# Attention, experts and a bilinear layer: the loop over further windows moved to the end of the program, with a buffer cleared ahead of the experts

## The chip, the cores and the metric

The kernel runs on one core of a Trainium2 chip. The metric is the device time of one execution in microseconds. The core's engines are named here as the profile names them: PE is TensorE, PEld its weight load, DVE is VectorE, ACT ScalarE, POOL GpSimd, SP SyncE, which issues most of the transfers.

## The reference

```python
# attention: batch 2, 8 heads, 768 tokens, 64 dims, 16 clusters
q_assign = np.argmax(np.einsum('bhsd,hcd->bhsc', q_n, c_n), axis=-1)
k_assign = np.argmax(np.einsum('bhsd,hcd->bhsc', k_n, c_n), axis=-1)
mask = q_assign[:, :, :, None] == k_assign[:, :, None, :]
scores = scale * np.matmul(q, k.transpose(0, 1, 3, 2))
scores = np.where(mask, scores, -1000000000.0)
...
return np.matmul(attn, v).astype(np.float32)

# experts: x [1536, 512], w_gate [512, 8], w1 [8, 512, 1024], w2 [8, 1024, 512]
logits = x @ w_gate
expert_idx = np.argmax(logits, axis=1)
...
for e in range(E):
    mask = expert_idx == e
    xe = x[mask]
    h = np.maximum(xe @ w1[e], 0.0)
    ye = h @ w2[e]
    out[mask] = gate_w[mask, None] * ye

# bilinear layer: w_a, w_b [512, 1536], w_out [1536, 512]
a = x @ w_a
b = x @ w_b
return (a * b @ w_out).astype(np.float32)
```

## The kernel before

Three stages follow one another. The attention takes up to about 295 us. The experts take from there to 520 us, the bilinear layer from 526 us to the end. Every product runs as three products of float32r parts: high by high, high by low, low by high. So each weight chunk is loaded (`piece_load`, L97), for the last layer turned from 64-bit into 32-bit words by three VectorE instructions (`piece_bits`, L120 to L124), and then split (`piece_parts`): `hi` is a cast on ScalarE (L137), `lo` a subtraction `raw - hi` (L141), for every second chunk on GpSimd, for the others on VectorE. NRAW staging tiles `raw` take turns; a load waits until the `lo` that read the tile before it is done.

The tokens of each expert stand in a region of their own of `xs` in DRAM. GpSimd puts them there by indirect scatters (L508). An expert's first 256 tokens are one window (`window`, L961 on): eight blocks of hidden units, each 12 matmuls into one of three banks `h` (L968), then `hh` by ScalarE (L972) and `hl` by VectorE (L973), which reads the bank last and so frees it for the block three further on; then 96 matmuls `y` (L983) with the second weight. Chunks 0 to 3 of an expert are its first weight, two blocks to a chunk, 4 to 7 its second. Between the blocks, `tick` lets other work be put into the engines' queues, in the order in which the program is written: the next splits (`advance`), and, in the first window, steps of `tables` on VectorE (L600 to L694), which count tokens and make the tables of windows. `store` (L991, L992) copies `y` to its tokens' columns in `yt`, which holds all tokens' rows, transposed, for the last layer: 4 x 1792 float32 in each partition.

An expert with more than 256 tokens has further windows of 128 rows. The first of them, over all experts, is worked off by `spill` within the row of experts. Any others are taken by a loop on the device, `tc.For_i(0, nv)` (L1158), between the experts and the bilinear layer, one window to a pass, written into `yt`. With the inputs timed here the experts have 198, 119, 169, 188, 162, 192, 206 and 302 tokens, so there is one further window, `spill` takes it, and `nv` is 0. Ahead of the loop two small matmuls are issued (`keep_warm`, L701).

The bilinear layer splits columns of `yt` into `yh` and `yl` (L1212 and L1214, L1218), multiplies by `w_a` and `w_b` into `ab` (L1242), multiplies the two into `ga` (L1249), splits that into `gh` and `gl` (L1250, L1251) and multiplies by `w_out` into `o` (L1265). Rows of the result, scaled by the gate (L1273), are scattered to their tokens' places in `out` (L1276) by GpSimd.

Within an engine instructions run in the order in which they were issued. Between engines they wait for semaphores, which the framework places where tiles are read and written, or where a tile's memory was used by another before.

Of the kernel before, what the change touches and what calls it, by code (L numbers as in the profile page):

```python
# [8 lines left out]
F32 = mybir.dt.float32  # L9
# [15 lines left out]
WS = 128  # L25
# [4 lines left out]
def cluster_attention__then__moe__then__bilinear_kernel(  # L30
# [37 lines left out]
    # ---- weights in chunks of [128, 1024], each split into two float32r parts  # L68
# [7 lines left out]
    # A piece is what one staging tile holds: a chunk of w1 (256 columns) or of  # L76
    # w2 (256 rows), or half a chunk of w_a, w_b or w_out, which come as float64
    # and are read as pairs of 32-bit words.
# [25 lines left out]

    def piece_bits(n):
        """First part of a split: float64 to float32."""
        t = raw_t.pop(n)
        i, j = pieces[n]
        if j == 0:
            s = i % NSLOT  # L110
            pn = pools["a" if s < NA else "b"]
            hi_t[i] = pn.tile([128, CH], F32R, tag=f"hi{s}", name=f"hi_{i}")
            lo_t[i] = pn.tile([128, CH], F32R, tag=f"lo{s}", name=f"lo_{i}")
        if i >= MOE2:
            # float64 to float32: sign and top exponent bit stay, the other three
            # bits by which the exponents differ go, the fraction is cut to 23 bits
            # (exact for zeros, and to 24 bits in float32's normal range)
            r = t.rearrange("p (f w) -> p f w", w=2)
            tmp = pools["b"].tile([128, CH // 2], U32, tag="tmp", name=f"tmp_{n}", bufs=2)
            nc.vector.tensor_scalar(out=tmp, in0=r[:, :, 1], scalar1=5, scalar2=2,  # L120
                                    op0=ALU.logical_shift_left, op1=ALU.logical_shift_right)
            nc.vector.scalar_tensor_tensor(out=tmp, in0=r[:, :, 1], scalar=0xC0000000, in1=tmp,  # L122
                                           op0=ALU.bitwise_and, op1=ALU.bitwise_or)
            nc.vector.scalar_tensor_tensor(out=tmp, in0=r[:, :, 0], scalar=29, in1=tmp,  # L124
                                           op0=ALU.logical_shift_right, op1=ALU.bitwise_or)
            t = tmp
        bits_t[n] = t.bitcast(F32)

    def piece_parts(n, hi_eng, lo_eng):
        """Second part of a split: high and low float32r."""  # L130
# [16 lines left out]
    # ---- scratch in DRAM: a region of S*B rows for each expert  # L147
# [4 lines left out]
    # ---- constants of the routing  # L152
# [121 lines left out]
    # centroids over their norms, laid out as a block diagonal for each head pair  # L274
# [31 lines left out]
    # The norm of a query or key row scales its similarities by one positive  # L306
    # factor, so it does not change which centroid has the largest one.
    class Prep:
        """The steps that lay out the operands of a pair of heads."""
# [17 lines left out]
        def sims(self, tag="X", bufs=1):  # L327
            # similarities, transposed: row 32 g + 16 h + c
# [29 lines left out]
        def rows(self, nm, tag="X", bufs=1, copies=(act_copy, dve_copy, act_copy, dve_copy)):  # L358
            # cluster rows of the queries, penalty rows of the keys
# [21 lines left out]
        def high(self, nm, h, i, other, copy):  # L381
            """High parts: those of head h, in stack i, own half or (keys) the other one."""
# [63 lines left out]
    def pv_steps(p, g, j0=0, nj=NG, tags=("O", "X"), per=1):  # L446
        """Values times probabilities for nj query tiles of a group, in steps."""
# [22 lines left out]
    def emit_x(p, t0, nj, ot, sm, tag):  # L470
        b, hp = pairs[p]
        if hp == 0 and t0 == 0:
            xb[b] = xpool.tile([128, NT, DM], F32, name=f"x{b}")
            lg[b] = xpool.tile([128, NT, E], F32, name=f"lg{b}")
# [21 lines left out]
    # =========================== routing ===========================  # L496
# [4 lines left out]
    def apart(group, inst, why):  # L501
        """Scatters of a group go to rows of their own: none waits for another."""
# [104 lines left out]
        # the expert with the most tokens, and where its further window starts  # L607
# [21 lines left out]
        # all windows beyond the first, one to a partition  # L629
# [28 lines left out]
        # start of each window inside its expert, then the three columns of the table  # L658
# [16 lines left out]
        # where the tokens go: number and squared gate of each  # L675
# [135 lines left out]
    def place_split(t, c0, c1, copy):  # L811
        """Columns of tile t in two float32r parts."""
# [11 lines left out]
    def place_mm(t, d):  # L824
        """Adds the tokens of tile t to the transposed rows of the first window."""
# [75 lines left out]
    # =========================== experts ===========================  # L901
    st_yt = ExitStack()
    ytp = pool(ctx, "yt")
    yt = ytp.tile([128, DB, NTOK + W], F32, name="yt")
    pb = pool(ctx, "chunks_b")
# [7 lines left out]
    def advance(n, engines, later=0):  # L913
        """Splits up to piece n, of the last ones only the first part, and loads."""
# [31 lines left out]
    def win_xt(w, n, a):  # L946
        """Transposes of the rows 128 a ... of a window, and their split."""
# [48 lines left out]
    def spill(w, c0, tick, nxt):  # L996
        """A window of 128 rows with the rows stationary; returns its last part."""
# [98 lines left out]
    # the first banks are those that the first window's rows are read from until late  # L1096
# [53 lines left out]
    keep_warm(2, "xt", [128, 512], 2, mps)  # L1150
    st_me.close()

    # ---- any further windows, one at a time
    with ExitStack() as st:
        lp = pool(st, "loop")
        lps = pool(st, "loop_ps", space=PSUM)
        nv = nc.values_load(regs["ni"][0:1, 0:1], min_val=0, max_val=16, skip_runtime_bounds_check_because=why)
        with tc.For_i(0, nv) as it:  # L1158
            row = lp.tile([1, 4], I32, name="row")
            nc.sync.dma_start(out=row, in_=tab[bass.ds(it, 1)])  # L1160
            ev2 = sp_value(row[0:1, 0:1], E - 1)
            rv2 = sp_value(row[0:1, 1:2], E * NTOK - WS)
            dv2 = sp_value(row[0:1, 2:3], NTOK - WS)
            x1 = lp.tile([128, DM], F32, name="x1")
            nc.sync.dma_start(out=x1, in_=xs[bass.ds(rv2, WS)])
            x1t = lp.tile([128, DB, WS], F32, name="x1t")
            for d in range(DB):
                xp = lps.tile([128, 512], F32, tag="xp", name="xp")
                nc.tensor.transpose(xp[:, 0:128], x1[:, 128 * d:128 * d + 128], ident)
                nc.vector.tensor_copy(x1t[:, d, :], xp[:, 0:128])  # L1170
            h1 = lp.tile([128, FB, WS], F32, name="h1")
            for c in range(4):
                wt = lp.tile([128, DB, 256], F32, tag="wt", name="wt", bufs=2)
                nc.sync.dma_start(out=wt, in_=w1[bass.ds(ev2, 1), :, 256 * c:256 * c + 256].rearrange(
                    "e (k p) f -> p (e k) f", p=128))
                for j in range(2):
                    hp_ = lps.tile([128, 512], F32, tag="xp", name="hp")
                    for d in range(DB):
                        nc.tensor.matmul(hp_[:, 0:WS], lhsT=wt[:, d, 128 * j:128 * j + 128], rhs=x1t[:, d, :],
                                         start=(d == 0), stop=(d == DB - 1))  # L1180
                    nc.scalar.activation(out=h1[:, 2 * c + j, :], in_=hp_[:, 0:WS], func=AF.Relu)
            y1 = [lps.tile([128, 512], F32, tag=f"y1{d}", name=f"y1{d}") for d in range(DB)]
            for c in range(4):
# [121 lines left out]
```

## Time and profile before

| | |
|---|---|
| median of 3 runs | 832.33 us (831.39 to 832.38) |
| span of the profiled execution | 830.4 us |
| PE busy | 793.5 us, 96% |
| DVE busy | 541.5 us, 65% |
| ACT busy | 367.1 us, 44% |
| POOL busy | 292.9 us, 35% |
| transfers | 81.91 MB, mean 99 GB/s |

The span runs from the first to the last instruction of one profiled execution; the time of a run is taken around it. A share is an average over all three stages.

### The profile page before, as it was taken

Reading aid. Unit: us, or ns where it says so; the run is one execution under the profiler, and the core shown is the slowest. Engines: PE = TensorE matmul, PEld = TensorE weight load, DVE = VectorE, ACT = ScalarE, POOL = GpSimd, SP = SyncE. Lnnn points to the kernel's source line nnn. Section 1 sums busy time; section 2 is a strip of 40 time slices with the busy share of each in tenths; the row PEclk is TensorE's granted clock in tenths of the full one; section 3 lists DMA queues with packets and bytes.
Section 4 is the critical chain, followed back from the end, with each engine's and each line's share of the span. In section 5 each row is a group of like instructions: output and inputs, shape, how many; then the busy total and the mean of one; then the engine's idle time right before and its main releaser. Section 6 shows DMA issues by size and latency. Waiting matters only on the chain. (4 is left out here: it accounts for less than half of the span.)

```text
span 830.4 us, 12569 instructions
## 1 busy us (share of the span) xinstructions
PE 793.5 (96%) x4832; PEld 639.1 (77%) x4832; DVE 541.5 (65%) x900; ACT 367.1 (44%) x693; POOL 292.9 (35%) x233
## 2 busy tenths in 40 slices
PE   8999999999999988899999999799999999999996
PEld 5666666665666778899999999588888888888885
DVE  6868879778786789555554459874565667624333
ACT  5867667766676454445564542222322212201100
POOL 4915434344540454576553334321121121101011
PEclk9999999999999999799999999899999999999998
DMA  9405012221100155768785654431131120001011
GB/s 299 97 1 159 1 39 63 64 58 45 52 20 1 50 197 167 225 148 221 230 276 184 218 183 153 117 114 51 51 93 60 51 70 32 1 0 51 1 51 51
DMA packets 69949, 81.91 MB, mean 99 GB/s; under 512 B 27264, under 2 KB 48256, under 8 KB 69888
## 3 DMA queue, kind: packets, MB, share of 16 engines
q1 hardware_dynamic: 67584, 74.78, 30.5%
q0 software_dynamic: 2304, 6.31, 2.0%
q8 instruction: 39, 0.64, 0.3%
q14 instruction: 22, 0.18, 0.1%
HBM read 70.58 MB, written 10.50 MB: 98 GB/s over the span
## 5 line engine op out<-in xcount | busy, mean ns | idle before, releaser
L141 POOL TENSOR_TENSOR lo<-raw,hi 128x1024 fp32r<-128x1024 f32 x37 | 92.7, 2509 | 88.8 <-ACT hi L137 43.6
L1242 PE MATMUL ab<-yh,hi 128*128 128x512 f32 x288 | 113.4, 394 | 6.0 <-ACT yh L1214 6.0
L141 POOL TENSOR_TENSOR lo<-tmp,hi 128x512 fp32r<-128x512 f32 x36 | 51.5, 1430 | 179.1 <-ACT hi L137 177.1
L1242 PE MATMUL ab<-yh,lo 128*128 128x512 f32 x288 | 113.1, 393 | 0.0
L1249 DVE TENSOR_TENSOR ga<-ga,ab 128x512 f32<-128x512 f32 x36 | 24.7, 685 | 127.3 <-PE ab L1242 104.4
L417 DVE TENSOR_REDUCE nm<-s 128x1 f32<-128x768 f32 x96 | 91.5, 953 | 17.9 <-PE s L415 12.4
L424 ACT ACTIVATE pr<-s,nm 128x768 f32<-128x768 f32 x96 | 87.2, 908 | 17.6 <-DVE nm L417 16.5
L438 PEld LDWEIGHTS t<-ident,pr 128*128 128x128 f32 x576 | 62.9, 140 | 40.6 <-ACT pr L424 16.8
L415 PE MATMUL s<-ks,qs 128*128 128x512 f32 (+1 forms) x384 | 91.2, 359 | 1.1 <-ACT pr L424 0.6
L438 PE MATMUL t<-ident,pr 128*128 128x128 f32 x576 | 83.8, 279 | 2.8 <-DVE pt L444 2.8
L1248 ACT COPY ga<-ab 128x512 f32<-128x512 f32 x36 | 21.1, 587 | 143.3 <-PE ab L1242 143.3
L453 PE MATMUL o<-pt,vn 128*64 128x384 f32 (+1 forms) x432 | 82.5, 472 | 0.0
L968 PE MATMUL h<-xh,hi 128*128 128x256 f32 x256 | 68.3, 297 | 10.2 <-DVE hl L973 10.0
L137 ACT CAST hi<-raw 128x1024 fp32r<-128x1024 f32 x70 | 72.4, 1047 | 12.6 <-DMA raw<-in_moe_w 12.5
L1242 PE MATMUL ab<-yl,hi 128*128 128x512 f32 x288 | 77.8, 392 | 0.0
L983 PE MATMUL y<-hh,hi 128*128 128x256 f32 x256 | 73.5, 287 | 0.0
L141 DVE TENSOR_TENSOR lo<-raw,hi 128x1024 fp32r<-128x1024 f32 x35 | 61.0, 1746 | 18.0 <-ACT hi L137 17.5
L983 PE MATMUL y<-hh,lo 128*128 128x256 f32 x256 | 72.4, 283 | 0.0
L983 PE MATMUL y<-hl,hi 128*128 128x256 f32 x256 | 72.4, 283 | 0.0
L442 ACT COPY pt<-t 128x384 f32<-128x384 f32 x98 | 46.9, 480 | 54.4 <-PE t L438 52.7
L1242 PEld LDWEIGHTS ab<-yh,hi 128*128 128x128 f32 x288 | 54.8, 190 | 17.6 <-ACT yh L1214 6.2
L415 PEld LDWEIGHTS s<-ks,qs 128*128 128x128 f32 x384 | 58.2, 189 | 12.1 <-issue 3.8
(309 smaller groups left out, 1682.3 us busy)
## 6 DMA issues: line engine op xcount, KB each, us to landing
raw<-in_moe_w SPq DMA_DIRECT2D x72, 512.0 KB, 4.6
raw<-in_moe_w_a SPq DMA_DIRECT2D x12, 512.0 KB, 3.7
raw<-in_moe_w_b SPq DMA_DIRECT2D x12, 512.0 KB, 3.7
raw<-in_moe_w_out SPq DMA_DIRECT2D x12, 512.0 KB, 3.3
xs<-zero SPq DMA_DIRECT2D x8, 512.0 KB, 5.2
xw<-xs SPq DMA_DIRECT2D x15, 256.0 KB, 5.5
vn<-in_v SPq DMA_DIRECT2D x8, 384.0 KB, 3.2
qn<-in_q SPq DMA_DIRECT2D x14, 192.0 KB, 4.8
```

The source lines that it names most:

```text
L137: nc.scalar.copy(out=hi, in_=raw)
L141: eng.tensor_tensor(out=lo, in0=raw, in1=hi.bitcast(F32), op=ALU.subtract)
L415: nc.tensor.matmul(sc[:, c0:c1], lhsT=w, rhs=ks[s, h][:, i, c0:c1], start=(i == 0), stop=(i == 1))
L417: nc.vector.tensor_reduce(out=nm, in_=sc[:, 0:S], axis=AX.X, op=ALU.max, negate=True)
L424: nc.scalar.activation(out=pr, in_=sc[:, 0:S], func=AF.Exp, bias=nm, scale=1.0, accum_out=sums[p][:, t, h:h + 1])
L438: nc.tensor.transpose(x[:, 128 * n:128 * n + 128], pr[:, 128 * kb:128 * kb + 128], ident)
L442: nc.scalar.copy(out=dst, in_=src)
L453: nc.tensor.matmul(o[64 * h:64 * h + 64, 0:n], lhsT=vn[:, h, kb, :], rhs=pt_t[p, g, h][:, kb, 128 * j0:128 * j0 + n], start=(kb == 0), sto ...
L968: nc.tensor.matmul(hp_[:, 0:n], lhsT=a_[:, d, f0:f0 + 128], rhs=b_[:, d, 0:n], start=(i == 0), stop=(i == len(seq) - 1))
L983: nc.tensor.matmul(y[:, d, 0:n], lhsT=a_[:, fb % 2, 128 * d:128 * d + 128], rhs=b_[:, 0:n], start=(fb == 0 and d % 2 == 0 and i == 0), sto ...
L1242: nc.tensor.matmul(p_, lhsT=a_[:, d, f0:f0 + 128], rhs=b_[d], start=(i == 0), stop=(i == len(seq) - 1))
L1249: nc.vector.tensor_tensor(out=ga, in0=ga, in1=ab[1], op=ALU.mult)
```

## The change

The loop over further windows, with the load of its count, leaves its place between the experts and the bilinear layer and stands behind the last instruction of that layer, whose pools are closed first. As the layer is over by then, each pass takes its window through `w_a`, `w_b` and `w_out` itself and scatters its rows to `out`; the conversion of 64-bit words became a function for that (`to_f32`, the same three instructions). The two matmuls of `keep_warm` ahead of the loop are gone. `yt` is cleared with zeros by GpSimd right after it is allocated. `lg`, the routing's logits, comes from the pool of constants and no longer from the pool of the attention's output, whose memory `yt` takes. Comments were removed too.

```diff
+    def to_f32(out, in_):
...
+        r = in_.rearrange("p (f w) -> p f w", w=2)
+        nc.vector.tensor_scalar(out=out, in0=r[:, :, 1], scalar1=5, scalar2=2,
+                                op0=ALU.logical_shift_left, op1=ALU.logical_shift_right)
...
-            lg[b] = xpool.tile([128, NT, E], F32, name=f"lg{b}")
+            lg[b] = cp.tile([128, NT, E], F32, name=f"lg{b}")
...
     yt = ytp.tile([128, DB, NTOK + W], F32, name="yt")
+
+    nc.gpsimd.memset(yt, 0.0)
...
-    keep_warm(2, "xt", [128, 512], 2, mps)
     st_me.close()
...
-    with ExitStack() as st:
-        lp = pool(st, "loop")
-        lps = pool(st, "loop_ps", space=PSUM)
-        nv = nc.values_load(regs["ni"][0:1, 0:1], min_val=0, max_val=16, skip_runtime_bounds_check_because=why)
-        with tc.For_i(0, nv) as it:
-            row = lp.tile([1, 4], I32, name="row")
-            nc.sync.dma_start(out=row, in_=tab[bass.ds(it, 1)])
...
-            nc.sync.dma_start(out=yt[:, :, bass.ds(dv2, WS)], in_=y1s)
...
+    st_bil = ExitStack()
+    bp = pool(st_bil, "bil")
+    bps = pool(st_bil, "bil_ps", space=PSUM)
...
+    st_bil.close()
...
+    with ExitStack() as st:
+        lp = pool(st, "loop")
+        lps = pool(st, "loop_ps", space=PSUM)
+        nv = nc.values_load(regs["ni"][0:1, 0:1], min_val=0, max_val=16, skip_runtime_bounds_check_because=why)
+        with tc.For_i(0, nv) as it:
+            row = lp.tile([1, 4], I32, name="row")
...
+            for f in range(FB2):
+                ab1 = []
+                for n, w in enumerate((w_a, w_b)):
+                    wt = weight(w[:, 256 * f:256 * f + 256].rearrange("(k p) f -> p k f", p=128), DB)
+                    p_ = lps.tile([128, 512], F32, tag=f"ab{n}", name=f"ab1{n}")
+                    for d in range(DB):
+                        nc.tensor.matmul(p_[:, 0:WS], lhsT=wt[:, 128 * d:128 * d + 128], rhs=y1s[:, d, :],
+                                         start=(d == 0), stop=(d == DB - 1))
+                    ab1.append(p_)
+                g1 = lp.tile([128, WS], F32, tag="g1", name="g1", bufs=2)
+                nc.scalar.copy(out=g1, in_=ab1[0][:, 0:WS])
+                nc.vector.tensor_tensor(out=g1, in0=g1, in1=ab1[1][:, 0:WS], op=ALU.mult)
+                wt = weight(w_out[128 * f:128 * f + 128, :].rearrange("(k p) d -> p k d", p=128), 1)
+                nc.tensor.matmul(o1, lhsT=g1, rhs=wt, start=(f == 0), stop=(f == FB2 - 1))
+            o1s = lp.tile([128, DM], F32, name="o1s")
+            nc.vector.tensor_scalar(out=o1s, in0=o1, scalar1=ai2.bitcast(F32)[:, 1:2], scalar2=None, op0=ALU.mult)
+            nc.gpsimd.indirect_dma_start(
+                out=out, out_offset=bass.IndirectOffsetOnAxis(ap=ai2[:, 0:1], axis=0),
+                in_=o1s, in_offset=None, bounds_check=NTOK - 1, oob_is_err=True)
```

GpSimd's instructions at the end of the attention and the start of the experts, before (`lo_2` is the low part of chunk 2, the third of the first expert):

```order
L508 DMA xs_70<-x1_2160,slot1_145 12288x512 [waits DMAHW7_49]
L508 DMA xs_70<-x1_2160,slot1_145 12288x512
L508 DMA xs_70<-x1_2160,slot1_145 12288x512 [waits DVE_49]
L141 TENSOR_TENSOR lo_2_3389<-raw_2_1068,hi_2_3388 128x1024 [waits PE_49,Activation_49]
L141 TENSOR_TENSOR lo_4_3407<-raw_4_1366,hi_4_3406 128x1024 [waits PE_49,Activation_49]
L141 TENSOR_TENSOR lo_6_3502<-raw_6_3392,hi_6_3501 128x1024 [waits DMAHW0_49,PE_49,Activation_49]
L141 TENSOR_TENSOR lo_8_3565<-raw_8_3410,hi_8_3564 128x1024 [waits DMAHW2_49,PE_49,Activation_49]
```

and with the change:

```order
L511 DMA xs_70<-x1_2160,slot1_145 12288x512 [waits DMAHW7_49]
L511 DMA xs_70<-x1_2160,slot1_145 12288x512
L511 DMA xs_70<-x1_2160,slot1_145 12288x512 [waits DVE_49]
L909 MEMSET yt_3381 128x7168 [waits DMASW2_49,DMASW3_49,DMASW1_49,DMASW6_49,DMASW0_49,DMASW7_49,PE_49,Pool_49]
L144 TENSOR_TENSOR lo_2_3390<-raw_2_1068,hi_2_3389 128x1024 [waits Activation_49]
L144 TENSOR_TENSOR lo_4_3408<-raw_4_1366,hi_4_3407 128x1024 [waits PE_49,Activation_49]
L144 TENSOR_TENSOR lo_6_3503<-raw_6_3393,hi_6_3502 128x1024 [waits DMAHW0_49,PE_49,Activation_49]
L144 TENSOR_TENSOR lo_8_3566<-raw_8_3411,hi_8_3565 128x1024 [waits DMAHW2_49,PE_49,Activation_49]
```

The clearing of `yt` stands between the last scatter into `xs` and `lo_2`; it waits for the transfers of the scatters (DMASW), and all later `lo` on GpSimd stand behind it.

VectorE's instructions in the first window, with the change (no row of them moved; `hl_2_3492` is the low part of block 2 of window 0; line numbers are those of the changed kernel, three higher than before, `offs`, `cnts`, `wm`, `we` are small tiles of `tables`):

```order
L144 TENSOR_TENSOR lo_3414<-raw_1736,hi_3413 128x1024
L978 SCALAR_TENSOR_TENSOR hl_0_3442<-h_0_3428,hh_0_3441 128x256
L978 SCALAR_TENSOR_TENSOR hl_1_3459<-h_1_3445,hh_1_3458 128x256
L603 MEMSET offs 128x8
L604 COPY offs<-cnt 128x7
L605 COPY cnts<-cnt 128x8
L607 CAST offi<-offs 128x8
L978 SCALAR_TENSOR_TENSOR hl_2_3492<-h_2_3478,hh_2_3491 128x256
L613 TENSOR_REDUCE wm<-cnts 128x1
L614 TENSOR_TENSOR we_3496<-cnts,wm 128x8
L615 TENSOR_TENSOR we_3496<-we_3496,efirst 128x8
L616 TENSOR_REDUCE wm<-we_3496 128x1
```

The rows between `hl` instructions are the steps of `tables`; the row of one `hl` cannot run before those ahead of it.

VectorE's instructions from the last copy into `yt` to the first split of the bilinear layer, before:

```order
L992 COPY yt<-y_5903 128x2x256
L1157 TENSOR_LOAD wni
L1158 COMPARE_AND_BRANCH
L1158 UNCONDITIONAL_BRANCH x2
...
L1158 REGISTER_ALU
L1158 COMPARE_AND_BRANCH
L1158 UNCONDITIONAL_BRANCH
L1212 CAST yh_0_1_6391<-yt 128x512
L1212 CAST yh_0_3_6397<-yt 128x512
L1218 TENSOR_TENSOR yl_0_0_6389<-yt,yh_0_0_6388 128x512
```

and with the change:

```order
L997 COPY yt<-y_5904 128x2x256
L1174 CAST yh_0_1_6229<-yt 128x512
L1174 CAST yh_0_3_6235<-yt 128x512
L1180 TENSOR_TENSOR yl_0_0_6227<-yt,yh_0_0_6226 128x512
L1180 TENSOR_TENSOR yl_0_1_6230<-yt,yh_0_1_6229 128x512
L1180 TENSOR_TENSOR yl_0_2_6233<-yt,yh_0_2_6232 128x512
```

Loading the count, the branches, the loop's body and its exit stood between the copy and the first cast; now the cast follows the copy.

GpSimd's instructions at the end of the program, with the change:

```order
L1238 DMA out<-part,ai 1536x512 [waits DMASW2_49,DVE_49]
L1238 DMA out<-part,ai 1536x512 [waits DMASW3_49,DVE_49]
L1249 TENSOR_LOAD wni [waits DVE_49]
L1250 COMPARE_AND_BRANCH
L1250 ISA [waits DMASW4_49]
L1250 UNCONDITIONAL_BRANCH
```

The load of the count and the branch now stand behind the last scatter of the output; before, that was GpSimd's last work.

## Rows read from the trace of the kernel before

**Rows 1.** The page: the span, and busy us, share and instructions of each engine.

```profile
span 830.4 us, 12569 instructions
PE 793.5 (96%) x4832; PEld 639.1 (77%) x4832; DVE 541.5 (65%) x900; ACT 367.1 (44%) x693; POOL 292.9 (35%) x233
```

**Rows 2.** Timeline at the seam: start, us, engine, line, work, count, [idle before, releaser].

```profile
521.28 0.68 DVE L992 COPY yt<-y 128x512 f32 x1
521.38 0.38 SPq L103 DMA_DIRECT2D raw<-in_moe_w_a  x1
525.63 1.14 ACT L1214 CAST yh<-yt 128x512 fp32r<-128x512 f32 x2 [5.10 <-SPq L1158]
525.73 0.76 DVE L1212 CAST yh<-yt 128x512 fp32r<-128x512 f32 x2 [3.78 <-SPq L1158]
526.30 0.80 PE L1242 MATMUL ab<-yh,hi 128*128 128x512 f32 x1 [6.01 <-ACT yh L1214]
```

**Rows 3.** Stretches: length; busy us (count) of PE, PEld, DVE, ACT, POOL; clock, DMA share, GB/s.

```profile
303.40:306.80 3.40, 3.40 (x16) 3.40 (x17) 3.15 (x12) 0.38 (x1) 2.17 (x1) 0.50 0.74 254
526.30:532.40 6.10, 6.10 (x15) 4.85 (x16) 6.00 (x10) 1.58 (x3) 1.46 (x1) 0.52 0.14 3
```

**Rows 4.** Timeline where the first stretch's blocks reach the output product.

```profile
538.40 1.66 DVE L1251 TENSOR_TENSOR gl<-ga,gh 128x512 fp32r<-128x512 f32 x1
540.27 0.40 PE L1265 MATMUL o<-hi,gl 128*128 128x512 f32 x1
```

**Rows 5.** Timeline of GpSimd in the first window of the experts.

```profile
295.02 0.98 POOL L508 DMA_INDIRECT xs<-x,slot  x1 [0.30 <-PE x0t L831]
296.02 4.76 POOL L141 TENSOR_TENSOR lo<-raw,hi 128x1024 fp32r<-128x1024 f32 x2
303.20 2.37 POOL L141 TENSOR_TENSOR lo<-raw,hi 128x1024 fp32r<-128x1024 f32 x1 [2.42 <-ACT hi L137]
```

**Rows 6.** The scatters into xs (L508): issue to landing.

```profile
DMA to landing us min/median/max: 2.7/2.7/3.1
```

**Rows 7.** Timeline of GpSimd at the start, two memsets.

```profile
1.77 0.20 POOL L253 MEMSET cblk<- 128x128 f32 x1
1.91 0.73 POOL L255 MEMSET ohp<- 128x768 f32 x1
```

**Rows 8.** Timeline of VectorE at the start, one cast twice.

```profile
1.96 1.09 DVE L269 CAST qs<-zero 64x768 fp32r<-64x768 f32 x1
3.94 0.55 DVE L269 CAST qs<-zero 64x768 fp32r<-64x768 f32 x1
```

**Rows 9.** Timeline of VectorE in the first window of the experts.

```profile
296.91 6.10 DVE L141 TENSOR_TENSOR lo<-raw,hi 128x1024 fp32r<-128x1024 f32 x2
304.00 1.60 DVE L604 CAST offi<-offs 128x8 int32<-128x8 f32 x1
306.78 0.42 DVE L973 SCALAR_TENSOR_TENSOR hl<-h,hh 128x256 fp32r<-128x256 f32 x1
308.48 0.42 DVE L973 SCALAR_TENSOR_TENSOR hl<-h,hh 128x256 fp32r<-128x256 f32 x1 [0.20 <-ACT hh L972]
```

**Rows 10.** Timeline of TensorE in the first window of the experts.

```profile
303.40 0.58 PE L968 MATMUL h<-xh,hi 128*128 128x256 f32 x1 [2.91 <-DVE hl L973]
309.30 0.28 PE L968 MATMUL h<-xh,hi 128*128 128x256 f32 x1
312.18 0.28 PE L983 MATMUL y<-hh,hi 128*128 128x256 f32 x1
```

**Rows 11.** The output scatters (L1276): ns, first and last start; landing.

```profile
L1276 POOL DMA_INDIRECT out<-part,ai x12: 970/977/1000, 757.7 to 825.3; - x12
DMA to landing us min/median/max: 2.7/2.7/2.8
```

**Rows 12.** The program's end (L1301) on GpSimd's queue: ns min/median/max, starts.

```profile
L1301 POOLq DRAIN  x3: 45/109/5576, 824.0 to 830.1; - x3
```

**Rows 13.** Timeline of TensorE in the second window of the experts.

```profile
335.03 0.58 PE L968 MATMUL h<-xh,hi 128*128 128x256 f32 x1 [3.63 <-DVE hl L973]
```

More of the change, by code (lines that the diff above doesn't have):

```diff
@@ L103, in piece_load @@
             nc.sync.dma_start(out=t.rearrange("p (k f) -> p k f", k=src.shape[1]), in_=src)
+    def to_f32(out, in_):
+        r = in_.rearrange("p (f w) -> p f w", w=2)
+        nc.vector.tensor_scalar(out=out, in0=r[:, :, 1], scalar1=5, scalar2=2,
+                                op0=ALU.logical_shift_left, op1=ALU.logical_shift_right)
+        nc.vector.scalar_tensor_tensor(out=out, in0=r[:, :, 1], scalar=0xC0000000, in1=out,
+                                       op0=ALU.bitwise_and, op1=ALU.bitwise_or)
+        nc.vector.scalar_tensor_tensor(out=out, in0=r[:, :, 0], scalar=29, in1=out,
+                                       op0=ALU.logical_shift_right, op1=ALU.bitwise_or)
     def piece_bits(n):
@@ L114, in piece_bits @@
         if i >= MOE2:
-            r = t.rearrange("p (f w) -> p f w", w=2)
             tmp = pools["b"].tile([128, CH // 2], U32, tag="tmp", name=f"tmp_{n}", bufs=2)
[L120 to L125, printed above, removed]
+            to_f32(tmp, t)
             t = tmp
@@ L1149, in cluster_attention__then__moe__then__bilinear_kernel @@
             store(y, W, ov[e])
-    keep_warm(2, "xt", [128, 512], 2, mps)
     st_me.close()
-    with ExitStack() as st:
-        lp = pool(st, "loop")
-        lps = pool(st, "loop_ps", space=PSUM)
-        nv = nc.values_load(regs["ni"][0:1, 0:1], min_val=0, max_val=16, skip_runtime_bounds_check_because=why)
-        with tc.For_i(0, nv) as it:
-            row = lp.tile([1, 4], I32, name="row")
-            nc.sync.dma_start(out=row, in_=tab[bass.ds(it, 1)])
[L1161 to L1183, printed above, removed]
-                wt = lp.tile([128, 2, DM], F32, tag="wt", name="wt2", bufs=2)
-                nc.sync.dma_start(out=wt, in_=w2[bass.ds(ev2, 1), 256 * c:256 * c + 256, :].rearrange(
-                    "e (k p) d -> p (e k) d", p=128))
-                for j in range(2):
-                    for d in range(DB):
-                        nc.tensor.matmul(y1[d][:, 0:WS], lhsT=wt[:, j, 128 * d:128 * d + 128], rhs=h1[:, 2 * c + j, :],
-                                         start=(c == 0 and j == 0), stop=(c == 3 and j == 1))
-            y1s = lp.tile([128, DB, WS], F32, name="y1s")
-            for d in range(DB):
-                nc.vector.tensor_copy(y1s[:, d, :], y1[d][:, 0:WS])
-            nc.sync.dma_start(out=yt[:, :, bass.ds(dv2, WS)], in_=y1s)
@@ L1197, in cluster_attention__then__moe__then__bilinear_kernel @@
-    bp = pool(ctx, "bil")
-    bps = pool(ctx, "bil_ps", space=PSUM)
+    st_bil = ExitStack()
+    bp = pool(st_bil, "bil")
+    bps = pool(st_bil, "bil_ps", space=PSUM)
     ai = cp.tile([128, NTOK // 128, 2], U32, name="ai")
@@ L1278, in cluster_attention__then__moe__then__bilinear_kernel, with weight @@
                         in_=dst, in_offset=None, bounds_check=NTOK - 1, oob_is_err=True), "each token has a row of its own")
+    st_bil.close()
[5 more added lines that the diff above has]
+            row = lp.tile([1, 4], I32, name="row")
+            nc.sync.dma_start(out=row, in_=tab[bass.ds(it, 1)])
+            ev2 = sp_value(row[0:1, 0:1], E - 1)
+            rv2 = sp_value(row[0:1, 1:2], E * NTOK - WS)
+            dv2 = sp_value(row[0:1, 2:3], NTOK - WS)
+            x1 = lp.tile([128, DM], F32, name="x1")
+            nc.sync.dma_start(out=x1, in_=xs[bass.ds(rv2, WS)])
+            ai2 = lp.tile([128, 2], U32, name="ai2")
+            with nc.allow_non_contiguous_dma(reason="two words to a token"):
+                nc.sync.dma_start(out=ai2, in_=aux[bass.ds(dv2, WS)])
+            x1t = lp.tile([128, DB, WS], F32, name="x1t")
+            for d in range(DB):
+                xp = lps.tile([128, 512], F32, tag="xp", name="xp")
+                nc.tensor.transpose(xp[:, 0:128], x1[:, 128 * d:128 * d + 128], ident)
+                nc.vector.tensor_copy(x1t[:, d, :], xp[:, 0:128])
+            h1 = lp.tile([128, FB, WS], F32, name="h1")
+            for c in range(4):
+                wt = lp.tile([128, DB, 256], F32, tag="wt", name="wt", bufs=2)
+                nc.sync.dma_start(out=wt, in_=w1[bass.ds(ev2, 1), :, 256 * c:256 * c + 256].rearrange(
+                    "e (k p) f -> p (e k) f", p=128))
+                for j in range(2):
+                    hp_ = lps.tile([128, 512], F32, tag="xp", name="hp")
+                    for d in range(DB):
+                        nc.tensor.matmul(hp_[:, 0:WS], lhsT=wt[:, d, 128 * j:128 * j + 128], rhs=x1t[:, d, :],
+                                         start=(d == 0), stop=(d == DB - 1))
+                    nc.scalar.activation(out=h1[:, 2 * c + j, :], in_=hp_[:, 0:WS], func=AF.Relu)
+            y1 = [lps.tile([128, 512], F32, tag=f"y1{d}", name=f"y1{d}") for d in range(DB)]
+            for c in range(4):
+                wt = lp.tile([128, 2, DM], F32, tag="wt", name="wt2", bufs=2)
+                nc.sync.dma_start(out=wt, in_=w2[bass.ds(ev2, 1), 256 * c:256 * c + 256, :].rearrange(
+                    "e (k p) d -> p (e k) d", p=128))
+                for j in range(2):
+                    for d in range(DB):
+                        nc.tensor.matmul(y1[d][:, 0:WS], lhsT=wt[:, j, 128 * d:128 * d + 128], rhs=h1[:, 2 * c + j, :],
+                                         start=(c == 0 and j == 0), stop=(c == 3 and j == 1))
+            y1s = lp.tile([128, DB, WS], F32, name="y1s")
+            for d in range(DB):
+                nc.vector.tensor_copy(y1s[:, d, :], y1[d][:, 0:WS])
+            o1 = lps.tile([128, 512], F32, tag="o1", name="o1")
+            def weight(src, nk):
+                t64 = lp.tile([128, CH], U32, tag="t64", name="t64", bufs=2)
+                nc.sync.dma_start(out=t64.rearrange("p (k f) -> p k f", k=nk), in_=src)
+                t32 = lp.tile([128, CH // 2], U32, tag="t32", name="t32", bufs=4)
+                to_f32(t32, t64)
+                return t32.bitcast(F32)
+            for f in range(FB2):
[3 more added lines that the diff above has]
+                    p_ = lps.tile([128, 512], F32, tag=f"ab{n}", name=f"ab1{n}")
+                    for d in range(DB):
+                        nc.tensor.matmul(p_[:, 0:WS], lhsT=wt[:, 128 * d:128 * d + 128], rhs=y1s[:, d, :],
+                                         start=(d == 0), stop=(d == DB - 1))
+                    ab1.append(p_)
[9 more added lines that the diff above has]
+                in_=o1s, in_offset=None, bounds_check=NTOK - 1, oob_is_err=True)
```

## The prediction

> **What bounds the kernel now.** The first thing to read is the page's busy table [rows 1]: TensorE is busy for 96% of an 830.4 us span, so a change pays or costs where it alters TensorE's few waits, and all other work is free until it makes TensorE wait. The list of waits and the timeline then give the places. Two of them are touched.
>
> The first is the seam between the experts and the bilinear layer [rows 2]. The last copy out of the experts (VectorE, L992) starts at 521.28 and lasts 0.68, so it ends at 521.96. Nothing more is computed until 525.63, when ScalarE starts `yh`, 5.10 us after its previous work; VectorE follows at 525.73 and TensorE's first `ab` at 526.30, after 6.01 us idle. The releaser named for the first two is L1158, the head of the loop over further windows. It runs no pass on these inputs (no row of its body is in the trace), but its exit waits for every engine and every queue, among them the weight load issued at 521.38.
>
> The second is the first window of the experts. TensorE waits there 2.91 us until 303.40 for VectorE's `hl` [rows 10], and `hl` is late because VectorE stood behind GpSimd: two `lo` subtractions on VectorE took 6.10 us together [rows 9] where two `lo` on GpSimd took 296.02 to 300.78 [rows 5]. One VectorE `lo` was thus held across two GpSimd instructions that follow each other directly.
>
> **The change part by part, the seam.** The loop, its `TENSOR_LOAD` and the two warm-up matmuls leave the seam. In the new order VectorE's `yh` stands right behind the copy L992, and the first `ab` behind the last `y`. VectorE can start `yh` at 521.97 instead of 525.73: 3.76 us earlier. Is this what TensorE gains? Two paths lead from there to the first `o` matmul that needs `gl` (540.27). VectorE works without a gap from 525.73 until `gl` ends at 538.40 + 1.66 = 540.06 [rows 4]: 14.33 us. TensorE works without a gap too, the first 6.10 us at half clock (granted 0.52, after the 6.01 us idle) [rows 3]. If the clock stays up after the shorter idle time, TensorE arrives earlier than VectorE and waits for `gl`; if it halves again, both arrive as they did, shifted. Either way VectorE's 14.33 us from 521.97 give 536.30. The gain is **3.8 us**; lower bound 3.0 (if a weight piece behind `yl` isn't there yet), upper bound 5.1 (ScalarE's own wait). Removing two warm-up matmuls is in it.
>
> **The loop at the end.** The twelve output scatters are unchanged; the last starts at 825.3 and lands 2.7 us later, at 828.0 [rows 11]. Behind it now stand the load of the count, a branch and an exit that waits for every queue. The load and branch lie under the 1.7 us that the landing still takes. GpSimd's final drain lasts 5.576 us from 824.0 [rows 12], to 829.6, so part of the exit hides there. Bounds 0 and 1.6 us (the drain's 829.6 less the landing's 828.0, if the drain must follow the exit's waits in full). At the seam the exit let ScalarE start 0.5 us after the load of 521.38 could have landed at about 525.1; I take **0.5 us**.
>
> **The memset.** On GpSimd it stands between the last scatter into `xs` and `lo_2`. It waits for the scatters to land: the last starts at 295.02 [rows 5], landing takes 2.7 to 3.1 us [rows 6], so about 298.0. Its price by the nearest rows: 128x128 in 0.20 us and 128x768 in 0.73 us [rows 7], that is 0.83 ns for one more element in a partition, so 7168 elements take about 6.0 us (an estimate from these rows, nine times past the larger one). It runs from 298.1 to 304.1. Then `lo_2`, `lo_4`, `lo_6` follow back to back: 4.76 + 2.37 = 7.13 us [rows 5], to 311.2, where before they were over at 305.57.
>
> Who waits? `lo_2` is needed by block 4 of the window's eight (numbered from 0), which can't start before 306.5 now. The larger price is again VectorE's. Its order is `hl0`, `hl1`, `CAST offi`, `hl2`, five small operations on the counts (L610 to L614), `hl3`, eight more, `hl4`. Each `hl` gives back one of three banks, so block 5 waits for `hl2`, block 6 for `hl3`, block 7 for `hl4`. `CAST offi`, on 8 elements, took 1.60 us [rows 9], until GpSimd's `lo_6` ended at 305.57. Now three `lo` in a row lie across L610 to L614, so whether VectorE slips one operation into each gap or none, the last of the five is over only at about 311.4 and `hl3` at 311.9 (before 306.78 + 0.42 = 307.20). Block 6 then starts at 312.0 against 309.30 [rows 10]: 2.7 us late. `hl4` began 1.70 us after `hl3` (308.48); with GpSimd idle block 7 starts at about 314.0, where before it stood halfway between 309.30 and the first `y` at 312.18 [rows 10], at 310.74, and the loss is **3.3 us**. If `lo_8` comes in just then, as its weights can only be loaded after `lo_2` has been read, its 2.4 us add to that: 5.7. TensorE's wait before block 7 would then be 2 to 3 us, like the 2.91 that was followed by half rate, and 16 matmuls in 3.40 us [rows 3] instead of 16 x 0.12 (24 stand between 309.30 and 312.18) cost 1.5 more: **7.2 us**. I take 5.5, nearer to the upper end, since the three conditions follow from one another. As TensorE is the bound behind this window, the loss stays.
>
> Does the memset itself hold VectorE? `CAST qs`, which started at 1.96, 0.05 after GpSimd's memset of `ohp`, took 1.09 us, and 0.55 later [rows 7, 8], so a cast is held by a memset. `lo_5`, a subtraction of two tiles, runs about 298.8, inside the memset; no row shows such a pair. If it isn't held it ends at 300.0 and block 3 starts near 301, earlier than before, which only lengthens the wait for `lo_2`. If held, it ends at 305.4. I take the first: the two-input operations that were held stood behind GpSimd operations that read tiles, which a memset doesn't; the other end is rival (a). The Trainium skill, SBUF — State Buffer, section Who interferes with whom, says that a VectorE operation with two SBUF inputs is blocked by GpSimd operations that read SBUF, not by those that only write; by this rule `lo_5` is free and the first end of this paragraph holds, with a loss of 5.5; by the other end it would be the 8 of rival (a).
>
> **Other edits.** The first copy into `yt` comes behind the window's `y` matmuls, long after the memset. `lg` in the constant pool changes no instruction; the weight loads 8 and 9 wait for `lo_2` and `lo_4`, with the window load of the next expert behind them on SyncE's queue, to about 309; its transposes stand in the middle of the `y` matmuls, which start at 312.18 before and later now, so that is hidden. Without that cover each microsecond would count.
>
> **The sum.** The profiled span of 830.4 is 1.9 us below the median of the three runs, 832.33, which I take for what lies around it. 832.3 - 3.8 + 0.5 + 5.5 = 834.5 us.
>
> **Rivals.** (a) *The memset holds two-input operations too*: `lo_5` and then `hl0` go past 305, block 3 starts near 306 instead of 303.40, and all later `hl` queue behind three or four `lo`: loss about 8, 837.0 us. For it: VectorE's `lo` was held for the whole of two GpSimd instructions. (b) *GpSimd is idle when `hl4` comes*: loss 3.3, 832.3 (831.5 to 833.0): no change. For it: before, GpSimd stood idle for long between its `lo`. (c) *Faster*: the memset is wide and may run at less than 0.83 ns an element. It decides at about half: with 3.0 us `lo_6` ends at 308.3, `hl3` at 308.9, the loss is 1.7 and the time 830.5 to 830.7; at a third, 829.5. The same times come out if the second window gives the loss back: its 3.63 us wait for `hl` at 335.03 [rows 13] could shrink where VectorE arrives with the tables done. Against the first: the two rows leave little fixed cost (0.73 - 768 x 0.83 ns = 0.1 us) that would hide a faster rate; against the second: that wait too is behind GpSimd's `lo`, which are late now. (d) *The seam doesn't open*, because a weight piece is late there: 838.
>
> **Numbers.** 0.2% is 1.7 us; less is no change that a measurement here can tell. Main case 0.50 (833.0 to 836.1, slower in 9 of 10), (a) 0.10, (b) 0.20, (c) 0.17, (d) 0.03. Slower 0.45 + 0.10 + 0.03 = 0.58, same 0.05 + 0.20 = 0.25, faster 0.17. The range 830.0 to 837.3 leaves half of (c), (d) and some of (a) outside.
>
> **What the next profile would show.** One row `MEMSET yt` on GpSimd of about 6.0 us from about 298.1, then three `lo` to 311.2; TensorE's `y` of the first window at about 317.7 instead of 312.18; the seam with 2 to 3 us idle and the first `ab` 3.8 us nearer to the last `y`; loop rows only behind the last scatter. The prediction is wrong if the memset is much shorter than 6 us, if block 6 starts before 311, or if the last `y` of the experts is less than 3 us late.

## The result

The changed kernel takes 838.85 us (median of 14 runs, 836.79 to 844.92) against 833.48 us of the kernel before in the same measurement; the ratio is 1.0069 [1.0049, 1.0089]. On the 832.3 us of the prediction that is 838.1 us: slower, as forecast, but by 5.7 us and not by 2.2, and outside the range. The page of its profiled execution:

```profile
span 840.5 us, 12587 instructions
...
PE 795.2 (95%) x4828; PEld 636.8 (76%) x4828; DVE 546.4 (65%) x900; ACT 367.2 (44%) x693; POOL 295.9 (35%) x234
```

The span is 10.1 us longer than that of [rows 1], more than the medians of the runs differ. The profiled execution was one of the longer ones (842.54 us). Its attention started late: VectorE's first wait for the transposed `q` is 5.05 us long, 3.19 before, its next two waits are longer too, and the first `h` matmul of the experts started at 299.87 instead of 295.49. These 4.38 us are not the change's: in one execution of a kernel whose attention is that of before (e8 below) the first `h` came as late, at 299.66. All places below are therefore counted from the first `h` matmul, in us. `y` is that of the experts, the first one that of their first window; "end" is the time from the start of the last scatter to the end of the span:

| kernel | first `y` | last `y` | first `ab` | last scatter of `out` | end, after it |
|---|---|---|---|---|---|
| before | 16.69 | 224.08 | 230.81 | 529.84 | 5.07 |
| changed | 21.42 | 230.71 | 232.37 | 532.61 | 8.02 |

Four differences follow: the experts end 6.63 us later; the seam is 1.66 instead of 6.73 us long, 5.07 less; from the first `ab` to the last scatter 1.21 are lost again; the end is 2.95 longer. 6.63 - 5.07 + 1.21 + 2.95 = 5.72 us, which agrees with the timed difference.

**The first window.** GpSimd's timeline of the changed kernel (start, us, engine, line, work, count, [idle before, releaser]):

```profile
299.40 0.97 POOL L511 DMA_INDIRECT xs<-x,slot  x1 [0.31 <-issue]
302.73 6.08 POOL L909 MEMSET yt<- 128x7168 f32 x1 [2.36 <-PE h L973]
308.79 7.01 POOL L144 TENSOR_TENSOR lo<-raw,hi 128x1024 fp32r<-128x1024 f32 x3
316.18 2.38 POOL L144 TENSOR_TENSOR lo<-raw,hi 128x1024 fp32r<-128x1024 f32 x1 [0.38 <-ACT hi L140]
```

The view names a TensorE matmul as what released the memset. The last scatter starts at 299.40 and would have landed at 302.1 to 302.5 by the times of [rows 6], so its landing can have been what the memset waited for last; its start is, less 4.38, at 298.35 (forecast 298.1). The memset takes 6.08 us (forecast 6.0), and the three `lo` behind it end at 315.80; less 4.38 that is 311.4 (forecast 311.2). VectorE's timeline there:

```profile
303.23 1.23 DVE L144 TENSOR_TENSOR lo<-raw,hi 128x1024 fp32r<-128x1024 f32 x1 [0.72 <-ACT hi L140]
...
305.45 3.39 DVE L607 CAST offi<-offs 128x8 int32<-128x8 f32 x1
...
308.93 2.21 DVE L614 TENSOR_TENSOR we<-cnts,wm 128x8 f32<-128x8 f32 x1
311.17 2.30 DVE L615 TENSOR_TENSOR we<-we,efirst 128x8 f32<-128x8 f32 x1
...
313.70 2.12 DVE L617 TENSOR_TENSOR we<-we,wm 128x8 f32<-128x8 f32 x1
315.74 0.41 DVE L978 SCALAR_TENSOR_TENSOR hl<-h,hh 128x256 fp32r<-128x256 f32 x1
...
319.28 0.42 DVE L978 SCALAR_TENSOR_TENSOR hl<-h,hh 128x256 fp32r<-128x256 f32 x1
```

Three things are to be seen. The `lo` subtraction at 303.23 lies wholly inside the memset (302.73 to 308.81) and takes 1.23 us, as long as the last one ahead of the memset: it isn't held. The cast at 305.45 is, until 308.84. And of the small operations with two tiles (L614, L615, L617) each is held through one `lo` and slips in before the next: 2.21, 2.30, 2.12 us for 8 elements. The Trainium skill, SBUF — State Buffer, section Who interferes with whom, says that a cast can take the pair of ports that VectorE shares with GpSimd, and that an operation with two SBUF inputs contends with GpSimd instructions that read SBUF, not with those that only write it. The trace agrees with both: 3.39 us for the cast beside the memset, 1.23 for the subtraction beside it, 2.12 to 2.30 for the small operations beside `lo`. So `hl` of block 3 (315.74) starts at 311.4 when 4.38 are taken off, and TensorE waits:

```profile
311.17 0.49 PE L973 MATMUL h<-xh,lo 128*128 128x256 f32 x1 [4.52 <-POOL lo L144]
...
316.21 0.39 PE L973 MATMUL h<-xh,hi 128*128 128x256 f32 x1 [0.53 <-DVE hl L978]
...
319.75 0.39 PE L973 MATMUL h<-xh,hi 128*128 128x256 f32 x1 [1.86 <-DVE hl L978]
...
321.29 0.28 PE L988 MATMUL y<-hh,hi 128*128 128x256 f32 x1
```

Its wait for `lo_2` (4.52 us, up to 311.17) is followed by half clock, as the 2.91 us of [rows 10] were:

```profile
306.60:311.10 4.50, 0.06 (x1) 0.00 (x0) 4.42 (x4) 1.00 (x2) 4.50 (x3) 1.00 0.30 107
311.10:314.00 2.90, 2.83 (x13) 2.83 (x14) 2.80 (x4) 0.16 (x1) 2.90 (x3) 0.53 0.58 178
```

In the second row the granted clock is 0.53 (columns as in [rows 3]). Blocks 6 and 7 start at 316.21 and 319.75, the first `y` at 321.29: 4.73 us late.

**The second window** adds the other 1.9 us. TensorE's timeline there in the changed kernel, and GpSimd's row behind which VectorE stands:

```profile
343.94 0.39 PE L973 MATMUL h<-xh,hi 128*128 128x256 f32 x1 [3.64 <-DVE hl L978]
...
349.93 0.58 PE L973 MATMUL h<-xh,hi 128*128 128x256 f32 x1 [4.21 <-DVE hl L978]
```

```profile
343.77 4.68 POOL L144 TENSOR_TENSOR lo<-raw,hi 128x1024 fp32r<-128x1024 f32 x2
```

and the same places before:

```profile
338.72 0.58 PE L968 MATMUL h<-xh,hi 128*128 128x256 f32 x1 [0.76 <-DVE hl L973]
```

```profile
334.85 5.71 POOL L141 TENSOR_TENSOR lo<-raw,hi 128x1024 fp32r<-128x1024 f32 x2
```

The first wait is that of [rows 13]. The second one, 0.76 us before, has become 4.21. GpSimd's two `lo` lie without a gap now (4.68 us); before, VectorE's `lo` came in between them, and they took 5.71. Two kernels without clearing (e6, e8 below) go this slower way too, so a single profile doesn't show that the clearing is its cause.

**The seam** in the changed kernel:

```profile
532.24 0.50 PE L1204 MATMUL ab<-yh,hi 128*128 128x512 f32 x1 [1.38 <-ACT yh L1176]
532.31 0.68 DVE L997 COPY yt<-y 128x512 f32 x1
...
532.91 0.75 DVE L1174 CAST yh<-yt 128x512 fp32r<-128x512 f32 x2
...
545.55 1.65 DVE L1213 TENSOR_TENSOR gl<-ga,gh 128x512 fp32r<-128x512 f32 x1
...
547.26 0.50 PE L1227 MATMUL o<-hi,gl 128*128 128x512 f32 x1 [1.14 <-DVE gl L1213]
```

TensorE idles 1.38 us here instead of 6.01, but `gl` ends 14.29 us after VectorE's `yh` began (532.91 to 547.20; 14.33 before), and TensorE waits 1.14 us for it. That is most of the 1.21 us given back. The clock stays up this time: 1.00 in the 6.16 us from 532.24, where [rows 3] has 0.52 behind the long wait. 5.07 - 1.21 = 3.86 us are left.

**The end**, in the changed kernel: the exit's waits (L1250) on GpSimd, the program's end (L1340) and the last scatter:

```profile
L1250 POOLq EVENT_SEMAPHORE  x12: 42/43/2268, 833.2 to 836.4; - x12
```

```profile
L1340 POOLq DRAIN  x3: 45/103/3012, 836.7 to 840.2; - x3
```

```profile
832.48 0.97 POOL L1238 DMA_INDIRECT out<-part,ai  x1 [0.30 <-issue]
```

The last wait of the exit begins at 836.4, the drain at 836.7, and the drain takes 3.01 us. Before, one drain of 5.576 us [rows 12] began at 824.0, ahead of the last scatter's start, and ended 4.3 us after it, which is 3.3 us after that instruction was over on GpSimd (826.31); the landing, at about 828.0, lay under it. Now the drain begins only when the exit has seen the landing.

### The profile page after: what moved, and what is told of

Same layout as the page of the kernel before. It is cut to its first block, busy times and chain, and to the rows that moved or that the text cites. A ratio compares the mean times of both kernels' runs of the same rounds, so it can differ in the third digit from the quotient of the medians.

```text
span 840.5 us, 12587 instructions
## 1 busy us (share of the span) xinstructions
PE 795.2 (95%) x4828; PEld 636.8 (76%) x4828; DVE 546.4 (65%) x900; ACT 367.2 (44%) x693; POOL 295.9 (35%) x234
## 4 chain that ended last, share of the span: by engine, by line
PE 65%; DVE 14%; issue 12%; DMA 5%; ACT 1%; POOL 1%; SPq 0%; DVEq 0%; POOLq 0%; ACTq 0%
PE ab L1204 14%; PE y L988 8%; PE h L973 8%; PE o L456 7%; PE t L441 7%; PE o L1227 7%; PE s L418 7%; DMA out<-part,ai 4%; DVE nm L420 2%; DVE lo L144 2%; PE xo L481 2%; DVE tmp L112 1%; DVE pt L447 1%; PE sm L334 1%; DVE qs L306 1%
## 5 line engine op out<-in xcount | busy, mean ns | idle before, releaser
L144 POOL TENSOR_TENSOR lo<-raw,hi 128x1024 fp32r<-128x1024 f32 x37 | 89.8, 2431 | 90.2 <-ACT hi L140 40.6
L973 PE MATMUL h<-xh,lo 128*128 128x256 f32 x256 | 66.6, 291 | 4.5 <-POOL lo L144 4.5
```

The source lines that it names most:

```text
L144: eng.tensor_tensor(out=lo, in0=raw, in1=hi.bitcast(F32), op=ALU.subtract)
L973: nc.tensor.matmul(hp_[:, 0:n], lhsT=a_[:, d, f0:f0 + 128], rhs=b_[:, d, 0:n], start=(i == 0), stop=(i == len(seq) - 1))
```

## The experiments

Ratios are to the kernel before, run beside each on the same chip; the table has the places of one profile of each, counted as above. A profile is of one execution, and not always of a typical one: that of e4 is its fastest of 12 (831.43 us, median 836.05), as is that of e3 (826.62, median 828.61).

| kernel | ratio | first `y` | last `y` | first `ab` | last scatter | end |
|---|---|---|---|---|---|---|
| e1_no_memset | 0.9999 [0.9979, 1.0018] | 16.58 | 223.74 | 225.40 | 525.62 | 8.35 |
| e2_memset_alone | 1.0060 [1.0028, 1.0092] | 21.46 | 230.64 | 237.34 | 536.31 | 5.08 |
| e3_no_loop | 0.9962 [0.9937, 0.9987] | 16.66 | 221.76 | 223.42 | 523.65 | 5.03 |
| e4_memset_later | 1.0037 [1.0008, 1.0066] | 18.28 | 224.33 | 225.99 | 526.19 | 8.34 |
| e5_half_memset | 1.0030 [1.0008, 1.0052] | 16.46 | 227.85 | 229.51 | 529.73 | 7.93 |
| e6_second_loop | 1.0036 [1.0019, 1.0053] | 16.60 | 225.11 | 232.20 | 531.22 | 7.64 |
| e8_held_load | 0.9967 [0.9947, 0.9987] | 16.68 | 225.44 | 228.96 | 529.09 | 5.05 |
| e9_later_alone | 1.0034 [1.0014, 1.0054] | 20.01 | 228.37 | 235.00 | 534.04 | 5.06 |
| e10_act_clear | 1.0024 [1.0003, 1.0045] | 16.55 | 227.62 | 229.28 | 529.50 | 7.98 |

### The three parts, each by itself

e1_no_memset, the changed kernel:

```diff
-    nc.gpsimd.memset(yt, 0.0)
```

> The changed kernel without the clearing of yt. Theory: the change is a sum of three parts, the clearing +6.6 us (read between the two traces at the last y of the experts, 4.4 us of another start taken off), the seam -3.8, the loop at the end +3.0. Without the clearing -0.8 us against the kernel before, a ratio of 0.999. Rival: only the 4.7 us that are lost up to the first y of the first window belong to the clearing, the rest is the moved loop's: then +1.0 us, a ratio of 1.001, and the last y of the experts comes late here too.

Measured 0.9999: no difference that the interval could tell from the -0.1% of the theory or the +0.1% of the rival. The profile decides: first and last `y` stand where they did before (16.58, 223.74), so the rival is out. The only edit is the memset, so the 0.7% between this kernel and the changed one, 5.8 us, is the clearing's (each was timed against the kernel before, not against the other).

e2_memset_alone, the kernel before (with `lg` from `cp`):

```diff
+    nc.gpsimd.memset(yt, 0.0)
```

> The kernel before with the clearing of yt and lg in the constant pool, the loop and the warm-up matmuls where they were. Theory: +6.6 us, ratio 1.008, the seam and the end as before. Rival (4.7 us in the first window, the rest from the moved loop): +4.7, ratio 1.0056. Rival of the prediction (nothing else than the size of this term was wrong): 7.2 to 8 us, ratio 1.009 to 1.010.

Measured +0.60%, 5.0 us [2.3, 7.7], which leaves 4.7, 6.6 and 7.2 alike. The profile has the last `y` 6.56 us late without any moved loop, and the seam (6.70 us) and the end as before. So the loss behind the first window is not the moved loop's.

e3_no_loop, the changed kernel without clearing:

```diff
-    with ExitStack() as st:
-        lp = pool(st, "loop")
...
-        with tc.For_i(0, nv) as it:
...
```

> The changed kernel without the clearing and without the loop at the end (it leaves out further windows beyond the one that spill takes, of which these inputs have none). Theory: only the seam's gain is left, -3.8 us, ratio 0.9954, and 5.1 us from the last scatter to the end as before. Rival: the longer end is not the loop's but that of slower transfers in this execution; then the run without the clearing is as fast as this one.

Measured -0.38%, 3.2 us, and an end of 5.03 us. The run without the clearing alone (e1) isn't as fast, so the rival is out: the seam's gain is real, and the longer end is the loop's. In its profile the drain covers the landing again:

```profile
L1265 POOLq DRAIN  x3: 45/113/5587, 818.4 to 824.6; - x3
```

e6_second_loop, the kernel before:

```diff
+    with ExitStack() as st:
+        lp = pool(st, "loop2")
+        nv = nc.values_load(regs["ni"][0:1, 0:1], min_val=0, max_val=16, skip_runtime_bounds_check_because=why)
+        with tc.For_i(0, nv) as it:
+            row = lp.tile([1, 4], I32, name="row2")
+            nc.sync.dma_start(out=row, in_=tab[bass.ds(it, 1)])
```

> The kernel before with a second loop of the same count behind the last scatter (its body, one small load, doesn't run), the first left at the seam. Theory: the end grows from 5.1 to 8.0 us after the last scatter and nothing else moves: +3.0 us, ratio 1.0035. The prediction's value was +0.5 with a bound of 1.6.

Measured +0.36%, 3.0 us [1.6, 4.4], as expected; the end is 7.64 us, 2.6 longer than before. In this profile the last `y` is 1.0 us later than before, ahead of the added loop, so the two executions differ by more than the edit. The drain's row is that of the changed kernel, behind the exit's waits (L1283):

```profile
L1283 POOLq EVENT_SEMAPHORE  x12: 42/43/3292, 825.9 to 830.1; - x12
```

```profile
L1308 POOLq DRAIN  x3: 45/103/3012, 830.4 to 834.0; - x3
```

### The clearing: its place, its length, its engine

e4_memset_later (the changed kernel) and e9_later_alone (the kernel before) issue the clearing behind `lo_2` and `lo_4`:

```diff
-    nc.gpsimd.memset(yt, 0.0)
...
     advance(NA + NRAW, ENG)
+    nc.gpsimd.memset(yt, 0.0)
```

> The changed kernel with the same clearing issued behind lo_2 and lo_4 instead of ahead of them. Theory that its place costs: TensorE's wait for lo_2 goes, the cast offi is held to about 307 and hl3 behind lo_6 to about 310, so 1 to 2.5 us are left of the 6.6, and the time is +0.2 to +1.7 us against before. Rival, its 6 us of GpSimd and of VectorE's port are the price wherever it stands in this window: +5 to +6 us.

> The kernel before with the clearing issued behind lo_2 and lo_4 and lg in the constant pool, all else unchanged; to be held against the clearing ahead of lo_2 (+5.0 us, 1.0060, and 6.6 us late at the last y of its profile). Place theory, by the profile of the same place in the changed kernel: first y 1.6 us late, +0.2 to +2 us, ratio 1.000 to 1.0025. Duration theory, by that kernel's time (0.4% slower): +3.5 to +5 us, ratio 1.004 to 1.006.

The measured times lie between the two theories, and the intervals reach into both, so neither is shown nor out. Against e1 the first costs 0.38%, against the kernel before the second costs 0.34%: about 3 us each, somewhat more than half of the clearing at its old place, with intervals that overlap those of the changed kernel and of e2. GpSimd's timeline of e9:

```profile
296.12 4.76 POOL L141 TENSOR_TENSOR lo<-raw,hi 128x1024 fp32r<-128x1024 f32 x2
300.82 6.08 POOL L1094 MEMSET yt<- 128x7168 f32 x1
306.85 2.37 POOL L141 TENSOR_TENSOR lo<-raw,hi 128x1024 fp32r<-128x1024 f32 x1
```

`lo_2` and `lo_4` are in time again and so is block 4, but the memset and `lo_6` lie end to end on the small operations instead. The two profiles, though the work around is the same, differ by 1.7 us at the first `y` and by 4.0 at the last; that of e4 is the execution 4.6 us below its median.

e5_half_memset, the changed kernel:

```diff
-    nc.gpsimd.memset(yt, 0.0)
+    nc.gpsimd.memset(yt[:, 0:2, :], 0.0)
```

> The changed kernel with half of yt cleared, at the same place: 128x3584, so 3.0 us on GpSimd. Theory: what is late is the three lo behind it and with them hl3; their last ends 3 us sooner, the first y comes 1.7 us late instead of 4.7, and the whole is 3 us faster than the changed kernel: about +2.5 us against before, ratio 1.003. Rival: any clearing there puts the three lo back to back and costs the same: +5.7, ratio 1.007.

Measured +0.30%, as the theory's sum has it, but not by its steps: the first `y` isn't late at all (16.46), the last is by 3.8 us. In this profile all of the loss is in the second window. Why the first lost nothing can be read from the trace: TensorE waits there twice, 1.65 and 2.01 us, and the granted clock is 1.00 in the 3.4 us behind each, where the kernel before has one wait of 2.91 us [rows 10] and 3.40 us at 0.50 behind it [rows 3]:

```profile
305.08 0.39 PE L973 MATMUL h<-xh,lo 128*128 128x256 f32 x1 [1.65 <-POOL lo L144]
...
310.12 0.39 PE L973 MATMUL h<-xh,hi 128*128 128x256 f32 x1 [2.01 <-DVE hl L978]
```

e10_act_clear, the changed kernel, clearing by ScalarE:

```diff
-    nc.gpsimd.memset(yt, 0.0)
...
+            if w == 0 and fb in (1, 2, 3, 4):
+                nc.scalar.activation(out=yt[:, fb - 1, :].rearrange("p (a b) -> p a b", b=128),
+                                     in_=ident.unsqueeze(1).to_broadcast([128, (NTOK + W) // 128, 128]),
+                                     func=AF.Copy, scale=0.0)
```

> The changed kernel with yt cleared by ScalarE, four instructions of 128x1792 behind hh of blocks 1 to 4 of the first window, about 1.8 us each by the 0.59 us of a 512-wide copy. Theory: the price of the clearing is GpSimd's, whose lo come late and back to back and hold VectorE; on ScalarE it holds nobody but hh and hi behind it, so the first y is less than 1.5 us late and the time is that of the kernel without clearing, -0.5 to +1 us, ratio 0.999 to 1.001. Rival, writing 3.7 MB of yt in the middle of the first window costs whoever does it: first y 4 us late or more, ratio 1.005.

The rival is out: the first `y` is in time (16.55). The time is +0.24%, 2.0 us [0.3, 3.8], above the theory's +1 though the interval reaches below it, and the last `y` is 3.5 us late, which the theory has no step for. TensorE's first wait in the second window, 2.09 us before, is 4.16 here:

```profile
332.63 0.74 PE L972 MATMUL h<-xl,hi 128*128 128x256 f32 x4 [4.16 <-DVE xl L961]
```

### A better version

e8_held_load, the kernel before:

```diff
+    hold = [84]
...
-        while nload[0] < min(len(pieces), n + NRAW) and pieces[nload[0]] in chunk_src:
+        while nload[0] < min(len(pieces), n + NRAW, hold[0]) and pieces[nload[0]] in chunk_src:
...
+    hold[0] = len(pieces)
+    load_ahead(nsplit[0])
     bp = pool(ctx, "bil")
```

> The kernel before, loop at the seam, with the last weight load ahead of the loop (piece 84, issued at 521.38) held back until behind it. Theory: the 6 us at the seam are the landing of that load, for which the loop's exit waits; without it the exit comes at about 522.5, ScalarE's yh at 523 instead of 525.6, and the time falls by 2.5 us, ratio 0.997, with no cost at the end. Rival: the exit itself, its waits one after another on five engines, is the price: then no change, and only taking the loop away opens the seam.

Measured -0.33%, 2.8 us, as expected. The seam of its profile:

```profile
526.80 0.68 DVE L993 COPY yt<-y 128x512 f32 x1
527.95 1.14 ACT L1217 CAST yh<-yt 128x512 fp32r<-128x512 f32 x2 [1.90 <-SPq L1159]
528.62 0.50 PE L1245 MATMUL ab<-yh,hi 128*128 128x512 f32 x1 [2.80 <-ACT yh L1217]
...
529.06 0.39 SPq L103 DMA_DIRECT2D raw<-in_moe_w_a  x1
```

ScalarE waits 1.90 us for the exit instead of 5.10, TensorE 2.80 instead of 6.01, and the held load goes out behind the loop. So most of the wait was for the landing of that load; 1.90 us of waiting for the exit remain. This kernel is faster than the one before and the changed one, and leaves the loop where it was.

## Why the prediction missed

**The seam** was right: forecast 3.8 us, 3.86 in the profile, and by the step given, VectorE's 14.3 us from `yh` to `gl` as the bound, with TensorE there first, its clock up. e3 alone times it at 3.2 us [1.1, 5.2].

**The loop at the end** is the step that failed: "so part of the exit hides there ... I take 0.5 us", with a bound of 1.6. The drain was taken as a stretch with a fixed end, under which the exit's waits could lie. It is an instruction behind them in GpSimd's queue: it begins when they are done and then lasts 3.0 us. The moved loop cost 2.95 us at the end of the changed kernel, and a second loop 3.0 as timed in e6. Without the loop it began ahead of the last scatter, so that landing and drain overlapped; the row that showed this was there [rows 12] (5.576 us from 824.0), and was read for its end only. The upper bound should have been the drain put wholly behind the exit: 828.0 + 5.6 - 829.6 = 4.0 us, from the rows in hand. With 2.95 in place of 0.5 the prediction's sum is 837.0 us.

**The clearing** was right in its mechanism for the first window. Its length, its start, the end of the three `lo`, `hl` of block 3 (311.4 for a forecast 311.9 less the 0.42 that it lasts) all came as worked out. The half clock came behind the wait for `lo_2`, and TensorE waits for `hl` before blocks 6 and 7 all the same; behind the 1.86 us of wait before block 7, where the upper end of the forecast had put it, the granted clock was 1.00. So the first `y` was 4.73 us late where 5.5 was forecast. "As TensorE is the bound behind this window, the loss stays" isn't borne out by the two profiles: the loss grew by 1.9 us in the second window, to 6.6. But that growth is not shown to be the clearing's (below), and as timed the clearing costs 5.0 us (e2) or 5.8 (e1), on both sides of the 5.5 taken. Of the 3.6 us between 834.5 and 838.1, the profiles put 2.45 to the end and 1.1 to the clearing; the first is shown by e3 and e6, the second is no more than the timed interval leaves open (4.1 to 7.4 us for the whole change).

Of the rivals, (a) is out: `lo` inside the memset wasn't held. (b) didn't come: the next `lo` on GpSimd ran from 316.18 to 318.56, one small operation of VectorE (L622) was held beside it for 2.31 us, and `hl` of block 4 began 3.54 us after that of block 3, not 1.70. (c) is out with the memset's 6.08 us, (d) with the open seam.

**What stays open** is the second window. Five profiles without clearing have the first `y` within 0.11 us of each other and the last between 221.76 and 225.44. Where VectorE's `lo` gets in between GpSimd's two, TensorE's second wait there is 0.76 (before), 0.74 (e1) and 1.99 us (e3); where it doesn't, 3.05 (e6) and 3.04 (e8). So this window goes two ways of itself. From the first `y` of the first window to that of the second, the five take 32.61 (e3), 34.83 (e1), 34.86 (before), 36.21 (e6) and 36.47 us (e8). The kernels that clear take 33.57 (e4), 36.02 (e9), 36.85 (e2), 37.01 (changed), 38.74 (e10) and 39.03 (e5). The changed kernel is thus only 0.5 us above the slowest without clearing. All that clear, except e4 in its one profile, go the way without `lo` in between and have the last `y` 3.5 to 6.6 us later than the kernel before, though in two of them (e5, e10) the first window lost nothing. Whether the clearing makes the slower way more frequent isn't shown by one profile of each. Which work is late there, VectorE's tables or the splits, wasn't settled by a run of its own. Nor was what the two warm-up matmuls at the seam do by themselves.

## What to carry to other kernels

A loop over a count that is zero is not free where it stands: look at what its exit waits for. Holding back one load here gave about as much as taking the loop away (0.33% and 0.38%), and the moved loop gave back at the end most of what it had won, since it put the drain behind the last transfer. An instruction on an engine that is 35% busy can still cost about its own length (5.0 to 5.8 us timed for a memset of 6.08), if the work behind it holds a second engine that TensorE waits for.

## Not expected of the hardware

GpSimd's drain at the end of the program took 3.01 us when it began behind the exit, with the last scatter landed (changed kernel, e1, e6), and 5.58 to 5.59 us when it began ahead of the last scatter's start (before, e3).
